# A retention layer with a gated two-layer product: queries loaded, cast and turned by pairs of chunks, their columns read as two runs

## The chip, the core and the metric

The kernel runs on one core of a Trainium2 chip. The metric is the device time of one execution in microseconds (us), lower being better; the kernel before takes 306.24 us (median of 3 runs). The core has TensorE (PE in the profile, with its weight loads as a row of their own, PEld), VectorE (DVE), ScalarE (ACT), GpSimd (POOL) and SyncE (SP), which here only issues DMAs. Each engine carries out its instructions in the order of the program and waits on semaphores for the others.

## The reference

For 8 batches, 8 heads, 576 positions and 64 dimensions per head:

```
scores = matmul(q, k^T) / sqrt(64)
ret    = scores * gamma[h] ** (i - j)   for i >= j, else 0     # gamma[h] = 1 - 2 ** (-5 - h)
x      = matmul(ret, v)                 # as [4608 positions, 512]
h      = x @ w_in                       # 512 -> 2048
out    = (h * clip(h + 3, 0, 6) / 6) @ w_out    # 2048 -> 512
```

The inputs and the output are float32; the kernel computes in float16 with float32 sums.

## The kernel before

**Work and blocks.** The 4608 positions are 9 blocks of 512. Block 0 holds the first 64 positions of all eight batches (functions with "heads" in their names); block kb >= 1 holds positions 64 to 575 of batch kb - 1, as four chunks of 128. Chunks are numbered c = 4 to 35.

**A chunk.** `load` (L167) issues three DMAs of 256 KB on SP's queue, for k, q and v, one position in a partition; four buffers of each are in rotation. `casts` (L177) makes float16 copies: ACT the keys (L185), POOL the queries and the values (L186, L187), each with the decay of its position, since gamma ** (i - j) is split into a factor for the query and one for the key. `transposes` (L190) turns keys and queries so that a head's 64 dimensions lie on the partitions. On TensorE that is eight matmuls with the identity into PSUM tiles ptk and ptq, and a copy by ACT (kT) or DVE (qT) at L198; otherwise it is one DMA transpose on SP's queue (L200). Before, queries of chunks under `PE_T` = 13 and keys of chunks under `PE_K` = 20 are turned by TensorE (L622, L636 to L638, L646).

A chunk is worked off in two steps of 64 positions. `scores` (L222) multiplies kT and qT into the PSUM tiles pa, `masked` (L241, DVE, L245) masks them, `states` (L264) multiplies keys and values into a state per step, `add` (L287) adds the states up on DVE (L290, L293) with a decay by POOL (L294), `past` (L296) copies them to float16 by ACT (L300 to L303). `cross_over` (L323) and `inner` (L327) multiply the turned queries with the past state and the masked scores with the values into the PSUM tiles po, and ACT copies po to xT (L346), which holds the block's x turned. From chunk 16 on, two chunks go together in `scores`, `states`, `cross` and `inner`.

**The two products.** `up_unit` (L446) multiplies w_in with xT in four pairs of matmuls (ph), ACT makes u (L469) and DVE g (L471). `down_plain` and, from block 2 on, `down_strassen` multiply g with w_out (pd, pm); the latter has side sums that DVE does (L486), of g and of w_out. All matmuls of the products go through `product` (L158), so they stand under L162.

**The order** of the instructions on each engine is written by hand. `go` (L649) reads plans of short codes: `c12` casts chunk 12 and fetches a later one, `t12` turns it on TensorE, `a12` are its scores, `s12` its states, `u12` adds them, `z12` copies them, `x12` are the cross products, `i12` the inner ones, `D4` four steps of the down product, `U1` an up unit, `L` and `R` up units of the left or right half of a block, `+1` a side sum. From block 2 on the tables STEADY and FIRST_STEADY say which codes follow which up unit. PSUM tiles named pp rotate through six buffers: a new one waits until the one six before it has been read.

Of the kernel before, what the change touches and what calls it, by code (L numbers as in the profile page):

```python
# [12 lines left out]
FP32 = mybir.dt.float32  # L13
FP16 = mybir.dt.float16
# [7 lines left out]
def kernel(  # L22
# [13 lines left out]
    P = 128  # L36
# [32 lines left out]
    ij = const.tile([P, NJ + 4], I32)  # L69
    fj = const.tile([P, NJ + 4], FP32)  # L70
    key, odd = fj[:, NJ + 1:NJ + 2], fj[:, NJ + 3:NJ + 4]
    arg = const.tile([P, NJ + 1, 2 * H], FP32)
    dec = const.tile([P, NJ + 1, 2 * H], FP32)
# [16 lines left out]
    def indices():  # L90
        nc.vector.memset(half, 0.5)
        nc.gpsimd.iota(ii[:, 0:NJ], pattern=[[0, NJ]], base=0, channel_multiplier=1)
        nc.gpsimd.iota(ii[:, NJ:NJ + 1], pattern=[[1, 1]], base=0, channel_multiplier=1)
        nc.gpsimd.iota(query, pattern=[[TL, 2], [1, NJ], [NJ, RP]], base=0, channel_multiplier=0,
                       allow_small_or_imprecise_dtypes=True)
        make_identity(nc, ident16)
        p_ = ii[:, NJ:NJ + 1]
        nc.vector.tensor_scalar(ij[:, 0:NJ], ii[:, 0:NJ], P - B, 1, ALU.bitwise_and, ALU.logical_shift_right)
        nc.vector.tensor_copy(ij[:, NJ:NJ + 1], p_)
        nc.vector.tensor_scalar(ij[:, NJ + 1:NJ + 2], p_, RP - 1, 2, ALU.bitwise_and, ALU.logical_shift_left)  # L100
        nc.vector.tensor_scalar(ij[:, NJ + 2:NJ + 3], p_, 5, None, ALU.logical_shift_right)
        nc.vector.tensor_scalar(ij[:, NJ + 3:NJ + 4], p_, 4, 1, ALU.logical_shift_right, ALU.bitwise_and)
        nc.vector.tensor_copy(fj, ij)
        nc.vector.tensor_tensor(fj[:, 0:NJ], fj[:, 0:NJ], query[:, 0:TL:RP], ALU.add)
        nc.vector.tensor_scalar(fj[:, NJ:NJ + 1], fj[:, NJ:NJ + 1], 1.0, -float(P // 2), ALU.mult, ALU.add)
        nc.vector.tensor_copy(by_chunk.rearrange("p (c e r) -> p c e r", c=NCB, e=2),
                              ident16.rearrange("p (r e c) -> p c e r", e=2, c=NCB))

    def distances():
        nc.vector.memset(scale, float(np.log(D ** -0.5)))  # L110
        nc.vector.tensor_tensor(key, key, fj[:, NJ + 2:NJ + 3], ALU.add)
# [12 lines left out]
    def decays():  # L124
        for h in range(H):
            lg = float(np.log(gamma[h]))
            nc.gpsimd.tensor_scalar(arg[:, :, h], fj[:, 0:NJ + 1], lg, float(np.log(D ** -0.5)),
                                    ALU.mult, ALU.add)
            nc.gpsimd.tensor_scalar(arg[:, :, H + h], fj[:, 0:NJ + 1], -lg, 0.0, ALU.mult, ALU.add)
# [13 lines left out]
    def mask_of_chunk():  # L143
        nc.gpsimd.memset(mask, 1.0)
        nc.gpsimd.affine_select(out=mask, in_=mask, compare_op=ALU.is_ge,
                                fill=0.0, base=0, pattern=[[1, P]], channel_multiplier=-1)
        nc.gpsimd.tensor_copy(mask[SUB:P, 0:SUB], mask[SUB:P, SUB:P])
# [18 lines left out]

    def load(c):  # L167
        tiles, dmas = [], []
        b, s0 = c // NCB - 1, TL + P * (c % NCB)
        for nm, src in (("k", k), ("q", q), ("v", v)):  # L170
            t = io.tile([P, H, D], FP32, tag=f"f{nm}", name=f"f{nm}{c}")
            dmas.append(nc.sync.dma_start(t, src[b, :, s0:s0 + P, :].rearrange("h s d -> s h d")))
            tiles.append(t)
        st[c] = dict(f=tiles)
        return dmas

    def casts(c):  # L177
        fk, fq, fv = st[c]["f"]
        dd = dec[:, NJ, :].unsqueeze(2).to_broadcast([P, 2 * H, D])
        k16 = work.tile([P, NP, 2, D], FP16, tag="k16", bufs=4, name=f"k16_{c}")  # L180
        q16 = work.tile([P, NP, 2, D], FP16, tag="q16", name=f"q16_{c}")
# [4 lines left out]
        nc.gpsimd.tensor_tensor(by_head(q16), in_rows(fq), in_rows(dd[:, 0:H, :]), ALU.mult)  # L186
        nc.gpsimd.tensor_tensor(v16, fv, dd[:, H:2 * H, :], ALU.mult)  # L187
        st[c].update(k16=k16, q16=q16, v16=v16)

    def transposes(c, on_pe, names="kq"):  # L190
        for nm in names:
            src = st[c][nm + "16"].rearrange("p i a d -> p (i a d)")
            dst = work.tile([P, NP, P], FP16, tag=f"{nm}T", bufs=dict(k=4, q=6)[nm], name=f"{nm}T_{c}")
            if on_pe:
                pt = psum.tile([P, NP, P], FP32, tag="pp", name=f"pt{nm}{c}")
                for i in range(NP):
                    product(pt[:, i, :], src[:, i * P:(i + 1) * P], ident16, start=True, stop=True)
                (nc.scalar.copy if nm == "k" else nc.vector.tensor_copy)(dst, pt)  # L198
            else:
                nc.sync.dma_start_transpose(dst, src)  # L200
            st[c][nm + "T"] = dst
# [9 lines left out]
    def mm(*args, **flags):  # L211
        return lambda: nc.tensor.matmul(*args, skip_group_check=True, **flags)  # L212

# [8 lines left out]
    def scores(c0):  # L222
# [6 lines left out]
        for x, c in enumerate(g):  # L229
            kT, qT = st[c]["kT"], st[c]["qT"]  # L230
# [77 lines left out]
    def cross(c0, flip):  # L308
# [5 lines left out]
        for x, c in enumerate(g):  # L314
            for i in range(NP):
                for a in range(2):
                    s, cc, b = a ^ flip, i // 2 + 2 * a, i % 2
                    todo[a].append(mm(gs[c0]["po"][s][rows(b), x, cc, :], z16s[c][rows(a), s, i, :],
                                      st[c]["qT"][rows(a), i, rows(s)],
                                      start=bool(flip) and x == 0 and i < 2, stop=False))  # L320
# [6 lines left out]
    def inner(c0):  # L327
# [16 lines left out]
        xt = xts[kb][:, :, i0 * P:i0 * P + n * P].rearrange("p n (x s q) -> p s x n q", x=n, s=2)  # L344
        for s in range(2):
            nc.scalar.copy(xt[:, s], po[s])  # L346
        for c in g:
            del st[c], z16s[c]
# [18 lines left out]
    def load_half(i, nm, e, queue, behind=None):  # L367

        if nm not in hd.setdefault(i, {}):
            if queue is nc.gpsimd:  # L370
                hd[i][nm] = heads16(i, nm)
            else:
                f = io.tile([P, H, D], FP32, tag=f"f{nm}", name=f"h{nm}{i}")
                hd[i][nm] = f.rearrange("p (e j) d -> p e j d", e=2)
# [6 lines left out]
    def heads16(i, nm):  # L381
        return work.tile([P, 2, NJ, D], FP16, tag=f"{nm}16", bufs=dict(k=4, q=3, v=NV16)[nm], name=f"h{nm}16_{i}")
# [6 lines left out]
    def turn_heads(i, nm, copy):  # L389
# [6 lines left out]
        t = work.tile([P, x, NJ, y], FP16, tag=f"{nm}T", bufs=dict(k=4, q=6)[nm], name=f"h{nm}T_{i}")  # L396
# [225 lines left out]
    PE_T, PE_K = 13, 20  # L622
# [9 lines left out]
    def cast(c):  # L632
        if c < NCH:
# [3 lines left out]
            if c >= PE_T:  # L637
                transposes(c, False, "kq" if c >= PE_K else "q")  # L638
            fetch(c + IOB + (c < PE_T - 2))

    def do(todo):
        for what, c in todo:
            if what == "+":
                side_sums(c)
            elif c < NCH:
                {"c": cast, "t": lambda c: transposes(c, True, "kq" if c < PE_T else "k"), "a": scores, "s": states, "u": add, "z": past,  # L646
# [33 lines left out]
    with tc.manual_schedule(engines={ENG.PE, ENG.DVE, ENG.Pool, ENG.Activation, ENG.SP}):  # L680
# [66 lines left out]
        for u in range(4, NFC):  # L747
# [5 lines left out]
           "x4 a5 s5 i4 u5 z5 D7 x5 D2 i5 D2 t6 L2 c7 a6 s6 u6 L3 z6 D1 t7 L3 D2 x6 a7 s7 i6 u7 z7 L3 c8 x7 D2 i7 L1 D3 "  # L753
# [70 lines left out]
```

## Time and profile before

| | |
|---|---|
| median of 3 runs | 306.24 us (305.5 to 306.63) |
| the profiled execution | 305.81 us, of which the span of the profile is 303.4 us |
| DMA queue of SP | 127552 packets, 40.65 MB |
| loads of q | 32 of 256 KB, 5.1 us each from issue to landing (median) |
| DMA transposes | 23 of queries (4.3 us to landing), 16 of keys (5.6 us) |
| DMA bytes in all | 46.95 MB, 155 GB/s over the span |

A row of a timeline gives the start, the duration of the group, the engine, the line, the operation with what it writes and reads, the number of instructions and, in brackets, how long the engine was idle before and what ended the wait. A row of the groups gives the busy time and the mean of one instruction in ns, then the idle time before. Matmuls overlap, so that eight of them in 0.26 us can start 0.09 us ahead of the next group. A row of the waits gives the sum in us, the number and the longest.

### The profile page before, as it was taken

To read this page: it belongs to the slowest core of one execution; us is meant where nothing else is said; L and a number is where in the kernel's file an instruction comes from. 1 tells how busy PE (TensorE), PEld (TensorE's weight loads), DVE (VectorE), ACT (ScalarE), POOL (GpSimd) and SP (SyncE) were. 2 spreads that over 40 slices of the span, in tenths; PEclk is the share of its full clock that TensorE was granted. 3 is DMA by queue.
4 is the path that set the end of the run, shared out by engine and by line. 5 is a ranking of instruction groups with operands and counts; after the bars stand their busy time and mean duration, and the time that the engine had idled before them with its cause. 6 is when DMAs were issued, how large, how long until landed. Compare 5 with 4: busy or idle time off the path is not lost.

```text
span 303.4 us, 12742 instructions
## 1 busy us (share of the span) xinstructions
PE 290.3 (96%) x5594; PEld 221.8 (73%) x5594; DVE 214.0 (71%) x385; ACT 196.7 (65%) x367; POOL 138.3 (46%) x176
## 2 busy tenths in 40 slices
PE   5799999999999899999999998999999999999995
PEld 2578565788655567878888776887788778787895
DVE  4729635878975668788977886779767885657554
ACT  4659965999677687675677566656755665555520
POOL 7885077607852900718633863187428203100510
PEclk9579999999999999999999999999999999999999
DMA  7999999998999999698999999999996200210113
GB/s 161 161 192 213 194 218 204 215 212 189 185 191 198 194 191 134 126 149 250 197 204 156 206 153 193 173 196 177 203 112 125 89 4 0 92 51 2 71 71 138
DMA packets 132758, 46.95 MB, mean 155 GB/s; under 512 B 121952, under 2 KB 128096, under 8 KB 132704
## 3 DMA queue, kind: packets, MB, share of 16 engines
q1 hardware_dynamic: 127552, 40.65, 75.6%
q0 software_dynamic: 4720, 5.11, 10.3%
q8 instruction: 43, 0.70, 1.1%
q10 hardware_dynamic: 432, 0.39, 0.6%
q14 instruction: 11, 0.09, 0.1%
HBM read 36.70 MB, written 9.44 MB: 152 GB/s over the span
## 4 chain that ended last, share of the span: by engine, by line
PE 87%; DVE 4%; ACT 4%; DMA 2%; issue 2%; SPq 0%; ACTq 0%; DVEq 0%
PE ph L162 38%; PE pm L162 28%; PE pd L162 9%; PE po L212 4%; PE pa L212 2%; DVE g L471 2%; DMA hq<-in_q_dram 2%; ACT u L469 1%; PE pu L212 1%; PE ptk L162 1%; PE hptq L393 1%; DVE a L245 1%; PE hpo L438 1%; ACT hqT L397 1%; ACT kT L198 1%
## 5 line engine op out<-in xcount | busy, mean ns | idle before, releaser
L162 PE MATMUL ph<-xT,win 128*64 128x512 f16 (+1 forms) x1248 | 146.7, 364 | 1.0 <-DVE z L290 0.6
L471 DVE SCALAR_TENSOR_TENSOR g<-u,ph 128x512 f16<-128x512 f32 (+1 forms) x156 | 98.3, 643 | 54.1 <-ACT u L469 53.8
L469 ACT ACTIVATE u<-ph,half 128x512 f32<-128x512 f32 (+1 forms) x156 | 100.2, 660 | 46.1 <-PE ph L162 43.4
L162 PEld LDWEIGHTS <-win 128*64 128x64 f16 x1248 | 85.4, 136 | 28.1 <-issue 2.5
L162 PEld LDWEIGHTS <-g 128*64 128x64 f16 x928 | 51.8, 110 | 14.6
L162 PEld LDWEIGHTS <-s 128*64 128x64 f16 x896 | 51.5, 110 | 8.6 <-issue 1.1
L294 POOL TENSOR_TENSOR z<-z,gpow 128x256 f32<-128x256 f32 x24 | 15.5, 646 | 76.3 <-DVE z L293 53.0
L162 PE MATMUL pm<-ws,s 128*64 128x256 f16 x672 | 46.8, 273 | 0.0
L187 POOL TENSOR_TENSOR v<-fv,dec 128x512 f16<-128x512 f32 x32 | 38.3, 1196 | 0.0
L186 POOL TENSOR_TENSOR q<-fq,dec 128x512 f16<-128x512 f32 x32 | 37.4, 1169 | 1.5 <-DMA fq<-in_q_dram 0.8
L550 POOL TENSOR_TENSOR u<-u,p 128x512 f32<-128x512 f32 x7 | 8.9, 1271 | 58.3 <-ACT u L590 52.0
L162 PE MATMUL pd<-wout,g 128*64 128x512 f16 x256 | 34.4, 382 | 0.0
L346 ACT CAST xT<-po 128x256 f16<-128x256 f32 (+1 forms) x44 | 18.6, 473 | 23.3 <-PE po L212 23.0
L162 PE MATMUL pm<-wout,g 128*64 128x256 f16 x448 | 32.0, 273 | 0.0
L245 DVE TENSOR_TENSOR a<-pa,mask 128x256 f16<-128x256 f32 (+1 forms) x44 | 21.9, 540 | 8.0 <-PE pa L212 6.6
L486 DVE TENSOR_TENSOR s<-g 128x1024 f16<-128x1024 f16 x28 | 21.5, 771 | 0.2
L185 ACT CAST k<-fk 128x512 f16<-128x512 f32 x32 | 19.9, 620 | 0.0
L300 ACT CAST z<-z 128x512 f16<-128x512 f32 x24 | 14.8, 618 | 4.7 <-DVE z L290 4.7
L162 PE MATMUL pm<-wout,s 128*64 128x256 f16 x224 | 16.7, 273 | 0.7 <-issue 0.6
L162 PE MATMUL pm<-ws,g 128*64 128x256 f16 x224 | 17.2, 274 | 0.0
L212 PE MATMUL po<-qT,z 64*64 64x64 f16 x512 | 12.4, 198 | 0.5 <-ACT z L303 0.2
L486 DVE TENSOR_TENSOR s<-g,s 128x1024 f16<-128x1024 f16 x14 | 12.7, 905 | 0.0
(109 smaller groups left out, 276.7 us busy)
## 6 DMA issues: line engine op xcount, KB each, us to landing
fk<-in_k_dram SPq DMA_DIRECT2D x32, 256.0 KB, 4.9
fq<-in_q_dram SPq DMA_DIRECT2D x32, 256.0 KB, 5.1
fv<-in_v_dram SPq DMA_DIRECT2D x32, 256.0 KB, 5.2
out_dram<-o SPq DMA_DIRECT2D x14, 512.0 KB, 4.4
wout<-in_moe_w_out_dram POOLq DMA_DIRECT2D x4, 512.0 KB, 16.9
out_dram<-o SPq DMA_DIRECT2D x7, 256.0 KB, 2.9
win<-in_moe_w_in_dram POOLq DMA_DIRECT2D x3, 512.0 KB, 10.7
hq<-in_q_dram SPq DMA_DIRECT2D x6, 128.0 KB, 5.2
```

The costliest lines, as they stand in the source:

```text
L162: nc.tensor.matmul(out[r], lhs[:, r], rhs, skip_group_check=True, **flags)
L185: nc.scalar.copy(by_head(k16), in_rows(fk))
L186: nc.gpsimd.tensor_tensor(by_head(q16), in_rows(fq), in_rows(dd[:, 0:H, :]), ALU.mult)
L187: nc.gpsimd.tensor_tensor(v16, fv, dd[:, H:2 * H, :], ALU.mult)
L212: return lambda: nc.tensor.matmul(*args, skip_group_check=True, **flags)
L245: nc.vector.tensor_tensor(a16[:, a, 0:n].rearrange("p x i q -> p (x i) q"), pa[a].rearrange("p x i q -> p (x i) q"), m, ALU.mult)
L294: nc.gpsimd.tensor_tensor(new, new, decay, ALU.mult)
L300: nc.scalar.copy(z16, zs[c])
L346: nc.scalar.copy(xt[:, s], po[s])
L469: nc.scalar.activation(uu[:, 0:n], ph[:, 0:n], ACTF.Relu, bias=half, scale=1.0 / 6.0)
L471: nc.vector.scalar_tensor_tensor(out=g[:, hf, ths, jr, :], in0=by_half(uu), scalar=1.0, in1=by_half(ph), op0=ALU.min, op1=ALU.mult)
L486: nc.vector.tensor_tensor(*pend.popleft())
```

## The change

The query load takes two chunks (c even, c + 1) in one DMA of 512 KB: partition p holds the positions 2p and 2p + 1 of the 256, so that a run in memory is 512 bytes instead of 256. POOL casts the two positions (e = 0, 1) in two instructions at the even chunk, each with its own column of decays, and then the even chunk's values; at the odd chunk it casts the values alone. The turned pair has its columns by e and then by partition, so that the 64 queries of a step are two runs of 32 columns. Scores and cross products take them in that order (`by_parity`), the mask is made for it, and ACT's copy to xT puts the positions back in their order by writing every second element.

`PE_T` becomes 14 and `PE_K` 17: TensorE turns the queries of chunks 4 to 13 (at the even chunk, both of the pair) and the keys of 4 to 16; a DMA transpose takes a pair of queries, 11 in all, and the keys of 17 to 35, 19 in all. Three places of the plan change. In the block of chunks 4 to 7, three `L` units go ahead of `z7` and one ahead of `x7`. `t13` goes ahead of `c15` and eight down steps, `t14` ahead of three up units, `t15` ahead of two up units and their down steps. Queries of block 0 share the tiles of the pairs (`half_tile`).

```diff
     def load(c):
-        tiles, dmas = [], []
+
+        dmas = []
         b, s0 = c // NCB - 1, TL + P * (c % NCB)
+        st[c] = {}
         for nm, src in (("k", k), ("q", q), ("v", v)):
-            t = io.tile([P, H, D], FP32, tag=f"f{nm}", name=f"f{nm}{c}")
-            dmas.append(nc.sync.dma_start(t, src[b, :, s0:s0 + P, :].rearrange("h s d -> s h d")))
-            tiles.append(t)
-        st[c] = dict(f=tiles)
+            if nm != "q":
+                t = io.tile([P, H, D], FP32, tag=f"f{nm}", name=f"f{nm}{c}")
+                dmas.append(nc.sync.dma_start(t, src[b, :, s0:s0 + P, :].rearrange("h s d -> s h d")))
+                st[c]["f" + nm] = t
+            elif c % 2 == 0:
+                t = io.tile([P, H, 2, D], FP32, tag="fq", bufs=2, name=f"fq{c}")
+                dmas.append(nc.sync.dma_start(t, src[b, :, s0:s0 + 2 * P, :].rearrange("h (p e) d -> p h e d", e=2)))
+                st[c]["fq"] = t
         return dmas
...
-        nc.scalar.copy(by_head(k16), in_rows(fk))
-        nc.gpsimd.tensor_tensor(by_head(q16), in_rows(fq), in_rows(dd[:, 0:H, :]), ALU.mult)
-        nc.gpsimd.tensor_tensor(v16, fv, dd[:, H:2 * H, :], ALU.mult)
+        nc.scalar.copy(by_head(k16), in_rows(st[c]["fk"]))
+        if c % 2 == 0:
+            q16 = work.tile([P, 2, NP, 2, D], FP16, tag="q16", bufs=2, name=f"q16_{c}")
+            for e in range(2):
+                nc.gpsimd.tensor_tensor(by_head(q16[:, e]), in_rows(st[c]["fq"][:, :, e, :]),
+                                        in_rows(dd[:, NJ + 1 + e, 0:H, :]), ALU.mult)
+            st[c]["q16"] = q16
+        nc.gpsimd.tensor_tensor(v16, st[c]["fv"], dd[:, NJ, H:2 * H, :], ALU.mult)
...
+            if nm == "q" and c % 2:
+                continue
+            n = dict(k=1, q=2)[nm]
...
+                for e in range(n):
+                    pt = psum.tile([P, NP, P], FP32, tag="pp", name=f"pt{nm}{c}_{e}")
+                    for i in range(NP):
+                        j = NP * e + i
+                        product(pt[:, i, :], src[:, j * P:(j + 1) * P], ident16, start=True, stop=True)
+                    (nc.scalar.copy if nm == "k" else nc.vector.tensor_copy)(dst[:, e], pt)
...
+                for x in range(2):
+                    qts[c + x] = dst[:, :, :, SUB * x:SUB * x + SUB].rearrange("p e i (s r) -> p i s e r", s=2)
...
+    by_parity = lambda t: t.rearrange("p (e r) -> p e r", e=2)
...
-                        todo[a].append(mm(pa[a][rows(s), x, i, :], kT[rows(a), i, rows(s)], qT[rows(a), i, rows(s)],
+                        todo[a].append(mm(by_parity(pa[a][rows(s), x, i, :]), kT[rows(a), i, rows(s)], qT[rows(a), i, s],
...
-        xt = xts[kb][:, :, i0 * P:i0 * P + n * P].rearrange("p n (x s q) -> p s x n q", x=n, s=2)
+        xt = xts[kb][:, :, i0 * P:i0 * P + n * P].rearrange("p n (x s r e) -> p s x n e r", x=n, s=2, e=2)
         for s in range(2):
-            nc.scalar.copy(xt[:, s], po[s])
+            nc.scalar.copy(xt[:, s], po[s].rearrange("p x n (e r) -> p x n e r", e=2))
...
-    PE_T, PE_K = 13, 20
+    PE_T, PE_K = 14, 17
...
-           "x4 a5 s5 i4 u5 z5 D7 x5 D2 i5 D2 t6 L2 c7 a6 s6 u6 L3 z6 D1 t7 L3 D2 x6 a7 s7 i6 u7 z7 L3 c8 x7 D2 i7 L1 D3 "
+           "x4 a5 s5 i4 u5 z5 D7 x5 D2 i5 D2 t6 L2 c7 a6 s6 u6 L3 z6 D1 t7 L3 D2 x6 a7 s7 i6 u7 L3 z7 c8 L1 x7 D2 i7 D3 "
...
-           "a12 s12 u12 c15 D4 z12 +1 D4 t13 x12 a13 s13 i12 u13 z13 D1",
+           "a12 s12 u12 t13 c15 D4 z12 +1 D4 x12 a13 s13 i12 u13 z13 D1",
...
-        go("U1 D3 U1 D2 U1 U1 D2 t14 x13 a14 s14 i13 u14 z14 o1 c16 U1 D2 U1 D2 U1 D2 U1 D2 +1 U1 t15 x14 a15 s15 i14 u15 z15 "
+        go("U1 D3 t14 U1 D2 U1 U1 D2 x13 a14 s14 i13 u14 z14 o1 c16 U1 D2 U1 D2 t15 U1 D2 U1 D2 +1 U1 x14 a15 s15 i14 u15 z15 "
```

More of the change, by code (lines that the diff above doesn't have):

```diff
@@ L68 @@
     ii = const.tile([P, NJ + 1], I32)
[L69 to L73, printed above, removed]
+    ij = const.tile([P, NJ + 6], I32)
+    fj = const.tile([P, NJ + 6], FP32)
+    key, odd = fj[:, NJ + 3:NJ + 4], fj[:, NJ + 5:NJ + 6]
+    arg = const.tile([P, NJ + 3, 2 * H], FP32)
+    dec = const.tile([P, NJ + 3, 2 * H], FP32)
     ident16 = const.tile([P, P], FP16)
@@ L110, in distances @@
         nc.vector.memset(scale, float(np.log(D ** -0.5)))
-        nc.vector.tensor_tensor(key, key, fj[:, NJ + 2:NJ + 3], ALU.add)
+        nc.vector.tensor_tensor(key, key, fj[:, NJ + 4:NJ + 5], ALU.add)
         nc.vector.scalar_tensor_tensor(out=key, in0=odd, scalar=float(TL), in1=key, op0=ALU.mult, op1=ALU.add)
@@ L190, in transposes @@
+        nc.gpsimd.tensor_tensor(v16, st[c]["fv"], dd[:, NJ, H:2 * H, :], ALU.mult)
+        st[c].update(k16=k16, v16=v16)
     def transposes(c, on_pe, names="kq"):
         for nm in names:
-            src = st[c][nm + "16"].rearrange("p i a d -> p (i a d)")
-            dst = work.tile([P, NP, P], FP16, tag=f"{nm}T", bufs=dict(k=4, q=6)[nm], name=f"{nm}T_{c}")
-            if on_pe:
[L195 to L198, printed above, removed]
-            else:
-                nc.sync.dma_start_transpose(dst, src)
@@ L206 @@
+            if nm == "k":
+                st[c]["kT"] = dst[:, 0]
+            else:
+                for x in range(2):
+                    qts[c + x] = dst[:, :, :, SUB * x:SUB * x + SUB].rearrange("p e i (s r) -> p i s e r", s=2)
+    qts = {}
     PAIRS = 16
@@ L229, in scores @@
         for x, c in enumerate(g):
-            kT, qT = st[c]["kT"], st[c]["qT"]
+            kT, qT = st[c]["kT"], qts[c]
             for i in range(NP):
@@ L372, in load_half @@
             else:
-                f = io.tile([P, H, D], FP32, tag=f"f{nm}", name=f"h{nm}{i}")
-                hd[i][nm] = f.rearrange("p (e j) d -> p e j d", e=2)
+                f = half_tile(io, "fq", i, FP32, "hq", bufs=2) if nm == "q" else io.tile(
+                    [P, H * D], FP32, tag=f"f{nm}", name=f"h{nm}{i}")
+                hd[i][nm] = f.rearrange("p (e j d) -> p e j d", e=2, j=NJ)
         d = queue.dma_start(hd[i][nm][:, e].rearrange("p j d -> p (j d)"),
@@ L395, in turn_heads @@
         x, y = (NCB, 2 * RP) if nm == "k" else (2 * NCB, RP)
-        t = work.tile([P, x, NJ, y], FP16, tag=f"{nm}T", bufs=dict(k=4, q=6)[nm], name=f"h{nm}T_{i}")
+        t = half_tile(work, "qT", i, FP16, "hqT", bufs=3) if nm == "q" else work.tile(
+            [P, H * D], FP16, tag="kT", bufs=4, name=f"hkT{i}")
+        t = t.rearrange("p (x j y) -> p x j y", x=x, j=NJ)
         copy(t, pt.rearrange("p j (x y) -> p x j y", y=y))
@@ L645, in do @@
             elif c < NCH:
-                {"c": cast, "t": lambda c: transposes(c, True, "kq" if c < PE_T else "k"), "a": scores, "s": states, "u": add, "z": past,
+                {"c": cast, "t": lambda c: transposes(c, True, "kq" if c < PE_T else "k" if c < PE_K else ""), "a": scores, "s": states, "u": add, "z": past,
                  "x": cross_over, "i": inner, "k": keys_heads, "h": head_states, "o": lambda _: store(*kept.popleft())}[what](c)
```

50 lines of the change are left out of this document (31 added, 19 removed).

## The prediction, made before the changed kernel had run

> **What bounds the kernel now.** I read the page first, then the table by stretches, then who waited for whom, then the timelines of TensorE (PE), VectorE (DVE) and ScalarE (ACT) around each wait. The first two lines are the page's busy times and its chain, then come two stretches (length, then busy time of PE, weight loads, DVE, ACT and POOL, granted clock, DMA share, GB/s), and three waits.
>
> ```profile
> PE 290.3 (96%) x5594; PEld 221.8 (73%) x5594; DVE 214.0 (71%) x385; ACT 196.7 (65%) x367; POOL 138.3 (46%) x176
> ...
> PE 87%; DVE 4%; ACT 4%; DMA 2%; issue 2%; SPq 0%; ACTq 0%; DVEq 0%
> ```
> ```profile
> 60.00:70.00 10.00, 9.30 (x221) 7.88 (x225) 7.92 (x21) 9.65 (x25) 2.51 (x4) 1.00 0.98 209
> ```
> ```profile
> 90.00:115.00 25.00, 23.66 (x380) 15.05 (x378) 15.69 (x27) 18.64 (x36) 9.90 (x11) 1.00 1.28 194
> ```
> ```profile
> POOL q L186 <- DMA fq<-in_q_dram: 0.8, 2, 0.6
> ...
> DVE hq L386 <- DMA hq<-in_q_dram: 2.6, 1, 2.6
> ```
> ```profile
> PE pa L212 <- ACT kT L198: 1.8, 3, 0.8
> ```
>
> PE is 96% busy and carries 87% of the chain: the kernel is bound by the number of PE instructions, and what else there is to win is PE's idle time. From 60 to 70 us ACT is busy for 9.65 of 10 and sets the pace. From 90 to 115 us PE idles 25.00 - 23.66 = 1.34 us, at full clock, and nearly all of it is one kind: scores that wait for ACT to copy a turned key (three waits, 1.8 us, two of them in this stretch). The DMA share of 1.28 looks alarming, yet GpSimd (POOL) waited for queries only 0.8 us in all. So fewer or longer query loads win nothing by themselves: I cost the new loads at nothing, hidden by loads that land ahead of their casts.
>
> **Term 1: the three waits for turned keys.** The change issues the turns of keys 13, 14 and 15 some units earlier. The rows are the cross products (po) and the scores (pa) behind them: first a pair without a wait, then the three with one.
>
> ```profile
> 76.06 0.26 PE L212 MATMUL po<-qT,z 64*64 64x64 f16 x8
> 76.15 0.30 PE L212 MATMUL pa<-qT,kT 64*64 64x64 f16 x16
> ...
> 87.09 0.26 PE L212 MATMUL po<-qT,z 64*64 64x64 f16 x8
> 87.83 0.32 PE L212 MATMUL pa<-qT,kT 64*64 64x64 f16 x16 [0.49 <-ACT kT L198]
> ...
> 93.93 0.26 PE L212 MATMUL po<-qT,z 64*64 64x64 f16 x8
> 94.68 0.32 PE L212 MATMUL pa<-qT,kT 64*64 64x64 f16 x16 [0.49 <-ACT kT L198]
> ...
> 101.67 0.26 PE L212 MATMUL po<-qT,z 64*64 64x64 f16 x8
> 102.78 0.32 PE L212 MATMUL pa<-qT,kT 64*64 64x64 f16 x16 [0.85 <-ACT kT L198]
> ```
>
> Without a wait the scores follow after 0.09 us. They follow after 0.74, 0.75 and 1.11 us at chunks 13, 14 and 15, so 0.65, 0.66 and 1.02 us are to be had. At chunk 13 something else is late next: the cross products there need the state that DVE adds, and DVE now casts two turned query tiles before that instead of one.
>
> ```profile
> 80.80 2.60 DVE L486 TENSOR_TENSOR ws<-wout,ws 128x1024 f16<-128x1024 f16 x2
> 83.45 0.69 DVE L198 CAST qT<-ptq 128x512 f16<-128x512 f32 x1
> 84.06 0.79 DVE L486 TENSOR_TENSOR ws<-wout 128x1024 f16<-128x1024 f16 x1
> ...
> 86.16 0.41 DVE L290 TENSOR_TENSOR z<-pa,zh 128x256 f32<-128x256 f32 x1
> ```
> ```profile
> 86.61 0.41 ACT L303 CAST z<-z 128x256 f16<-128x256 f32 x1 [0.26 <-DVE z L290]
> ```
>
> DVE runs without a gap here: the cast of 83.45 makes room at 84.06, so a second one costs 0.61. The add of 86.16 becomes 86.77, ACT's copy ends at 87.02 + 0.61 = 87.63, and the cross products of 87.09 start at about 87.70; the scores then at 87.79 against 87.83. Behind this new wait on PE stand the scores, states and inner products of chunks 12 and 13. So chunk 13 yields 0.04, and **term 1 is -(0.04 + 0.66 + 1.02) = -1.72**.
>
> **Term 2: turns that leave PE.** The keys of chunks 17, 18 and 19 go to the DMA; chunk 13's query comes onto PE, but under the wait just named, so it costs nothing there (0.22 if that wait were gone).
>
> ```profile
> 42.97 0.40 PE L162 MATMUL ptk<-ident,k 128*64 128x128 f16 x8
> 43.19 0.40 PE L162 MATMUL ptq<-ident,q 128*64 128x128 f16 x8
> ...
> 44.60 0.32 PE L212 MATMUL pa<-qT,kT 64*64 64x64 f16 x16
> ...
> 47.75 0.26 PE L212 MATMUL po<-qT,z 64*64 64x64 f16 x8 [0.20 <-ACT z L303]
> ```
>
> One turn of eight matmuls takes 43.19 - 42.97 = 0.22, and in the later stretch PE has no slack that would swallow it: **term 2 is -3 x 0.22 = -0.66**.
>
> **Term 3: two queries turned at once in front of the scores.** At chunk 4 PE turns key, query and now a second query, and DVE casts both before the scores may start.
>
> ```profile
> 43.62 0.69 DVE L198 CAST qT<-ptq 128x512 f16<-128x512 f32 x1 [1.13 <-PE ptq L162]
> ...
> 52.29 0.69 DVE L198 CAST qT<-ptq 128x512 f16<-128x512 f32 x1 [2.34 <-PE ptq L162]
> ```
> ```profile
> 53.05 0.32 PE L212 MATMUL pa<-qT,kT 64*64 64x64 f16 x16
> ...
> 55.30 0.41 PE L162 MATMUL ptq<-ident,q 128*64 128x128 f16 x8
> 55.66 1.53 PE L162 MATMUL ph<-xT,win 128*64 128x256 f16 x24
> ...
> 58.20 1.53 PE L162 MATMUL ph<-xT,win 128*64 128x256 f16 x24
> 59.91 0.26 PE L212 MATMUL po<-qT,z 64*64 64x64 f16 x8 [0.18 <-ACT z L300]
> ...
> 67.57 1.99 PE L162 MATMUL ph<-xT,win 128*64 128x256 f16 x32 [0.58 <-DVE z L290]
> ```
>
> Chunk 4: casts at 43.62 and 44.23, the second ends at 44.92, the scores go at 44.97 instead of 44.60: +0.37. That chunk 5's turn is shorter by 0.22 doesn't pay it back, since the cross products of 47.75 wait for a state that hangs on these scores. Chunk 6: casts at 52.29 and 52.90, the second ends at 53.59, scores at 53.64 instead of 53.05: +0.59; chunk 7's missing query returns 0.22, and the turn of 55.30 that lasts 0.36 instead of 0.22 (a PSUM tile not yet free) 0.14 more: +0.23. From chunk 8 on, three up units or an add stand between, and I count nothing.
>
> **Term 4: an order changed around chunk 7.** ACT copies the state after three activations instead of before them.
>
> ```profile
> 59.24 0.62 ACT L300 CAST z<-z 128x512 f16<-128x512 f32 x1 [0.27 <-DVE z L290]
> 59.76 1.20 ACT L469 ACTIVATE u<-ph,half 128x256 f32<-128x256 f32 x3
> ```
>
> The third activation needs the matmuls that end at 58.20 + 1.53 = 59.73; with its 0.40 (a third of 1.20) the copy starts at about 60.15, ends at 60.77, and the cross products of 59.91 go at about 60.80: +0.89. One up unit (1.53 / 3 less overlap, about 0.44) now stands ahead of them, net +0.45. Later chunk 9's query no longer takes a PSUM tile, so the wait of 0.58 at 67.57 should go: -0.57. **Terms 3 and 4: 0.37 + 0.23 + 0.45 - 0.57 = +0.48.**
>
> **Costed at nothing.** Three more tiny DVE instructions at the start hide under the 2.6 us wait for the first query; the wider decays and the mask lie in POOL's idle time. POOL casts both chunks of a pair at the even chunk, then its values: two casts in a row, the same number in all.
>
> ```profile
> L186 POOL TENSOR_TENSOR q<-fq,dec 128x512 f16<-128x512 f32 x32 | 37.4, 1169 | 1.5 <-DMA fq<-in_q_dram 0.8 <-PE po L212 0.7
> ```
> ```profile
> 83.91 2.92 SPq L200 DMA_TRANSPOSE qT<-q  x1
> ```
> ```profile
> qT<-q SPq DMA_TRANSPOSE x23, 4.3
> ```
>
> The values and the state decay queued behind come 1.2 us later at even chunks and earlier at odd ones; POOL is 46% busy. On SP's queue a transpose now waits for both casts, with the next loads behind it. Chunk 14's issue at 83.91 took 2.92; doubled 5.8, and 4.3 to land behind it at worst: 94.0, just where the scores at 94.68 - 0.7 want it. I take no wait there.
>
> Two costs are not in the trace: TensorE streams a query as two runs of 32 columns, and ACT writes xT at every second element.
>
> ```profile
> L406 PE MATMUL hpk<-hk,by_chunk 128*32 128x128 f16 x64 | 1.6, 222 | 0.0
> ...
> L162 PE MATMUL ptq<-ident,q 128*64 128x128 f16 x72 | 3.6, 219 | 0.0
> ...
> L346 ACT CAST xT<-po 128x256 f16<-128x256 f32 x24 | 7.8, 376 | 6.6 <-PE po L212 6.3
> ```
>
> Line 406 streams two runs of 64 and takes 222 ns, one run of 128 takes 219: 0 to 3 ns for each of 1024 matmuls, 0 to 3.1 us; I take 0, the end that line 406 is nearest to. The xT copy: 0, or twice its 376 ns; that would be on the path only where ACT is full, six copies about the stretch from 60 to 70 us, 0 to 2.3 us; I take 0. Neither can gain, as the elements are the same.
>
> **Sum**: -1.72 - 0.66 + 0.48 = -1.90. The profiled execution took 305.81 and would take 303.9; the median of the runs, 306.24, lies 0.43 higher: **304.3 us**.
>
> **The rivals.**
> (a) The waits are only passed on: ACT is full from 60 to 70 us, and freed PE time after 94 us meets the next copy of theirs. Then terms 1 and 3 cancel and term 2 or less is left: 305.6 to 306.5. For it speaks chunk 13, where it happens; against it the gaps of ACT and DVE after 90 us (DVE 15.69 of 25).
> (b) Slower: the two runs of columns cost TensorE. From 2 ns for each of 1024 matmuls the gain is gone, from 3.4 ns it is slower by over 0.5%. If each run counted as a matmul of its own, at 0.09 / 8 = 11 ns, it would be +11.5: 315.8. Against it speaks line 406.
> [...]
> (c) Chunk 14's queries land late in the crowded queue: the 0.66 of chunk 14 is lost and up to a us more: 304.3 + 0.66 to 304.3 + 1.66, about 305 to 306.
> (d) More: chunk 13 gives its 0.65 after all (303.7), and with 16 loads less a quarter of the chain's issue gaps goes too (2% of 303.4 is 6.1): 302.2 to 303.7.
>
> **How the numbers follow.** Forecast 0.51, (a) 0.24, (b) 0.13, (c) 0.05, (d) 0.07. 0.5% of 306.24, about what a measurement of this kernel tells from no change, is 1.5 us: faster means below 304.7, slower above 307.8. The forecast's own range is 303.3 to 305.2, so 0.44 of its 0.51 is faster, with (d) 0.51; same 0.07 + 0.24 + 0.05 = 0.36; slower 0.13. The range from 302.0 to 306.6 leaves out (b).
>
> **What would show it.** No row of scores with a wait for a turned key after 85 us; the cross products near 87 us with a wait for ACT's state copy; 24 matmuls fewer that turn keys (ptk) and 8 more that turn queries (ptq); about 0.4 us of new idle time near 45 and 54 us and 0.9 near 60, none near 67.6; pa and po no longer than before, and the copy of line 346 still at 376. Wrong: scores of chunks 14 to 17 that wait for a DMA, longer pa or po, or activations queued behind each other after 100 us.

## The result and the profile after

| | median, us | lowest to highest | runs | ratio to before, 95% interval |
|---|---|---|---|---|
| before | 306.33 | 305.50 to 306.63 | 4 | |
| changed | 302.54 | 302.52 to 303.87 | 4 | 0.9891 [0.9859, 0.9924] |
| changed, measured again beside its parts | 302.93 | 302.51 to 304.21 | 6 | 0.9907 [0.9876, 0.9938] (before there: 305.60, 25 runs) |

The change makes the kernel about 1% faster, 2.7 to 3.8 us, where 1.9 were forecast. A profiled execution of 302.57 us with a span of 300.6 is read here; before it was 305.81 with 303.4. Ratios leave disturbed runs out and are not formed from the two medians, so they can differ from the medians' ratio.

The page of the changed kernel, busy times and chain of waits:

```profile
PE 289.0 (96%) x5578; PEld 222.2 (74%) x5578; DVE 213.7 (71%) x389; ACT 197.9 (66%) x364; POOL 135.4 (45%) x176
...
PE 78%; DMA 10%; ACT 3%; DVE 2%; POOL 2%; issue 2%; SPq 1%; ACTq 0%
```

TensorE (PE) still is the bound, with 16 products fewer. Its waits in the changed kernel, by who ended them (sum in us, times, longest), and its two stretches (length, then busy time of PE, weight loads, DVE, ACT and POOL, clock, DMA share, GB/s):

```profile
PE pd L168 <- ACT o L556: 1.3, 2, 0.7
...
PE po L246 <- ACT z L336: 0.6, 1, 0.6
PE ph L168 <- ACT xT L382: 0.6, 1, 0.6
...
PE pa L246 <- DVE qT L226: 0.3, 1, 0.3
```
```profile
60.00:70.00 10.00, 9.10 (x213) 7.59 (x208) 7.57 (x19) 9.38 (x23) 1.00 (x3) 1.00 0.94 212
90.00:115.00 25.00, 24.86 (x389) 17.16 (x385) 16.98 (x30) 19.34 (x38) 10.04 (x11) 1.00 0.76 147
```

The wait of scores (pa) for a turned key is gone, and from 90 to 115 us PE idles 0.14 us in place of 1.34. New or longer are waits for ScalarE (ACT): for its copy of a finished output (o), of a state (z) and of xT. Around chunk 7, and at the scores of chunks 13 to 15:

```profile
57.93 0.33 PE L168 MATMUL ph<-xT,win 128*64 128x256 f16 x2
58.87 1.86 PE L168 MATMUL ph<-xT,win 128*64 128x256 f16 x30 [0.60 <-ACT xT L382]
61.36 0.25 PE L246 MATMUL po<-qT,z 64*64 64x64 f16 x8 [0.63 <-ACT z L336]
...
68.52 1.55 PE L168 MATMUL ph<-xT,win 128*64 128x256 f16 x24 [0.26 <-DVE z L326]
...
87.97 0.84 PE L168 MATMUL pd<-wout,g 128*64 128x512 f16 x6 [0.60 <-ACT o L556]
88.73 0.26 PE L246 MATMUL po<-qT,z 64*64 64x64 f16 x8
88.82 0.30 PE L246 MATMUL pa<-qT,kT 64*64 64x64 f16 x16
...
94.92 0.26 PE L246 MATMUL po<-qT,z 64*64 64x64 f16 x8
95.01 0.30 PE L246 MATMUL pa<-qT,kT 64*64 64x64 f16 x16
...
102.03 0.26 PE L246 MATMUL po<-qT,z 64*64 64x64 f16 x8
102.11 0.30 PE L246 MATMUL pa<-qT,kT 64*64 64x64 f16 x16
```

All three scores follow their cross products (po) after 0.09 us now. The operations themselves (mean ns is the last number ahead of the second bar):

```profile
L382 ACT CAST xT<-po 128x512 f16<-128x512 f32 x20 | 13.4, 741 | 16.4 <-PE po L246 16.4
...
L246 PE MATMUL po<-qT,z 64*64 64x64 f16 x512 | 12.5, 198 | 1.1 <-ACT z L336 0.6 <-ACT z L339 0.4
...
L382 ACT CAST xT<-po 128x256 f16<-128x256 f32 x24 | 9.2, 454 | 5.6 <-PE po L246 5.6
...
L246 PE MATMUL pa<-qT,kT 64*64 64x64 f16 x512 | 8.5, 195 | 0.5 <-DVE qT L226 0.3 <-DVE g L512 0.2
```

Products with two runs of columns last what they did (195 and 198 ns; 196 and 198 before). The copies of xT do not: 454 ns where it was 376, and 741 where it was 588.

**Where the time went.** To find the place of a difference I cut each trace at a score product of certain chunks (the first one of a chunk, but the ninth one of chunk 9 and of the pairs from 16 on; the same one in all kernels), so that the same work is compared whatever came earlier. Chunk 4 is counted from the start of the span; times in us, one profile each, up to the last score product's pair (34); behind it all kernels take 56.17 or 56.18 to PE's last product.

| kernel | to 4 | 4 to 9 | 9 to 13 | 13 to 16 | 16 to 20 | 20 to 34 |
|---|---|---|---|---|---|---|
| before | 44.60 | 25.41 | 17.83 | 28.93 | 22.51 | 104.59 |
| changed | 44.06 | 26.63 | 18.12 | 27.59 | 21.68 | 102.86 |
| difference | -0.54 | +1.22 | +0.29 | -1.34 | -0.83 | -1.73 |
| changed again | 45.48 | 26.62 | 18.12 | 27.61 | 22.63 | 102.18 |
| pairs alone | 45.05 | 26.70 | 17.99 | 28.93 | 22.47 | 103.69 |
| pairs and early turns | 45.90 | 26.63 | 18.13 | 28.06 | 22.55 | 103.16 |
| early turns alone | 45.42 | 25.42 | 17.96 | 27.92 | 22.88 | 103.22 |
| turns alone | 44.58 | 25.42 | 17.96 | 28.12 | 21.70 | 105.88 |
| turns alone, again | 43.93 | 25.40 | 19.89 | 27.45 | 21.89 | 105.44 |
| changed, xT contiguous | 46.01 | 26.44 | 18.12 | 27.76 | 22.61 | 101.57 |
| changed, old order at 7 | 45.77 | 26.70 | 18.12 | 27.74 | 22.60 | 101.58 |
| changed, halves | 44.38 | 25.81 | 18.12 | 27.47 | 22.58 | 102.54 |
| halves, xT contiguous | 44.87 | 25.73 | 18.12 | 27.68 | 21.97 | 102.98 |
| halves, old order at 7 | 45.19 | 25.63 | 18.12 | 27.66 | 21.67 | 102.30 |
| changed, later stream | 44.96 | 26.84 | 18.13 | 27.68 | 21.77 | 104.04 |

From chunk 4 to 16 kernels with the same program there agree within some hundredths to some tenths, so single profiles can be used there (the 19.89 holds a wait for a DMA, read below). Behind chunk 16 they don't: the two profiles of the changed kernel differ by 0.95 from 16 to 20. The start is another matter: kernels whose start is the same program reach chunk 4 anywhere between 44.06 and 46.01 us, so the 0.54 that the changed kernel seems to win there is chance. What is left is a loss of 1.51 up to chunk 13 and a win of 3.90 behind it, 1.73 of which lie where nothing was forecast. The second profile shows 2.41 there, but nothing of the 0.83.

### The profile page after: what moved, and what is told of

Read it like the earlier page. It is cut to its first block, busy times and chain, and to the rows that moved or that the text cites. A ratio compares the mean times of both kernels' runs of the same rounds, so it can differ in the third digit from the quotient of the medians.

```text
span 300.6 us, 12679 instructions
## 1 busy us (share of the span) xinstructions
PE 289.0 (96%) x5578; PEld 222.2 (74%) x5578; DVE 213.7 (71%) x389; ACT 197.9 (66%) x364; POOL 135.4 (45%) x176
## 4 chain that ended last, share of the span: by engine, by line
PE 78%; DMA 10%; ACT 3%; DVE 2%; POOL 2%; issue 2%; SPq 1%; ACTq 0%
PE ph L168 35%; PE pm L168 29%; PE pd L168 6%; DMA wout<-in_moe_w_out_dram 6%; PE po L246 4%; DMA hk<-in_k_dram 3%; PE pa L246 2%; DMA fk<-in_k_dram 2%; POOL win L658 1%; PE pu L246 1%; DVE g L512 1%; ACT u L510 1%; PE ptk L168 1%; POOL hv L412 1%; ACT k L203 1%
## 5 line engine op out<-in xcount | busy, mean ns | idle before, releaser
L168 PE MATMUL ph<-xT,win 128*64 128x512 f16 (+1 forms) x1248 | 145.1, 364 | 1.5 <-ACT xT L382 0.6
L168 PEld LDWEIGHTS <-s 128*64 128x64 f16 x896 | 50.3, 110 | 8.1 <-issue 0.2
L168 PE MATMUL pm<-ws,s 128*64 128x256 f16 x672 | 45.5, 273 | 0.0
L382 ACT CAST xT<-po 128x256 f16<-128x256 f32 (+1 forms) x44 | 22.5, 584 | 22.0 <-PE po L246 22.0
L210 POOL TENSOR_TENSOR v<-fv,dec 128x512 f16<-128x512 f32 x32 | 35.1, 1101 | 1.3 <-DMA fv<-in_v_dram 1.3
L527 DVE TENSOR_TENSOR s<-g 128x1024 f16<-128x1024 f16 x28 | 20.0, 716 | 0.2
L246 PEld LDWEIGHTS <-z 64*64 64x64 f16 x512 | 8.0, 106 | 7.7 <-ACT z L336 1.8
```

Source lines behind the costliest of these rows:

```text
L168: nc.tensor.matmul(out[r], lhs[:, r], rhs, skip_group_check=True, **flags)
L210: nc.gpsimd.tensor_tensor(v16, st[c]["fv"], dd[:, NJ, H:2 * H, :], ALU.mult)
L382: nc.scalar.copy(xt[:, s], po[s].rearrange("p x n (e r) -> p x n e r", e=2))
L527: nc.vector.tensor_tensor(*pend.popleft())
```

## The experiments

**Which part carries the gain.** The changed kernel with the old orders and with keys 17 to 19 on TensorE:

```diff
-    PE_T, PE_K = 14, 17
+    PE_T, PE_K = 14, 20
-  "... i6 u7 L3 z7 c8 L1 x7 D2 i7 D3 "   "... u12 t13 c15 D4 z12 +1 D4 x12 ..."   (and t14, t15)
+  "... i6 u7 z7 L3 c8 x7 D2 i7 L1 D3 "   "... u12 c15 D4 z12 +1 D4 t13 x12 ..."
```

> Pairs of queries alone: loaded, cast, turned and read in pairs as in the change, but the plan of the kernel before (turns of keys 13 to 15 and the state copy of chunk 7 where they were) and PE_K = 20. Theory S (the gain is the earlier key turns and the three key turns less on TensorE; the pairs themselves cost a little): 306.8 to 308.0, 0.5 to 1.7 above the kernel before, with the three waits for turned keys back (1.8 us). Theory D (the longer query loads, half the packets, bring most of it: an earlier start and fewer gaps late in the run): 303.5 to 305.

Measured: 306.63 (12 runs) beside 306.43, ratio 1.0007 [0.9976, 1.0038]. Queries by two bring nothing. That rules out D; by S it would have been 0.5 to 1.7 us above the kernel before, and it is 0.2. The kernel before, with the turns of 13 to 15 early and keys 17 to 19 turned by DMA:

```diff
-    PE_T, PE_K = 13, 20
+    PE_T, PE_K = 13, 17
-  "... c15 D4 z12 +1 D4 t13 x12 ..."   "U1 D3 U1 D2 U1 U1 D2 t14 x13 ..."   "... D2 +1 U1 t15 x14 ..."
+  "... t13 c15 D4 z12 +1 D4 x12 ..."   "U1 D3 t14 U1 D2 U1 U1 D2 x13 ..."   "... t15 U1 D2 U1 D2 +1 U1 x14 ..."
```

> The kernel before with only the earlier turns of keys 13, 14 and 15 and PE_K = 17; queries stay single, one DMA each. S: 306.3 - 0.65 - 0.66 - 1.02 - 0.66 = 303.3, since chunk 13's second query cast on VectorE isn't there. D: not below 304.8, and the start of the run and its second half as in the kernel before.

Measured: 305.14 (12 runs), 0.9970 [0.9936, 1.0004]. Less than S expected. The same without the DMA turns (only the three orders changed):

> The kernel before with only the earlier turns of keys 13, 14 and 15; PE_K stays 20. S: 306.3 - 2.33 = 304.0, 0.7 above the run with PE_K = 17. D: 305 to 306.

Measured: 306.19 (12 runs), 0.9960 [0.9918, 1.0002]; by the medians, 306.19 and 306.43, it is only 0.1%. So the parts brought 0 and at most 0.4%, with 1 inside every interval, and the whole 1.1%: either the whole was lucky, or it is more than its parts. The whole and the turns alone were run again, unaltered:

> The changed kernel a second time, unaltered, beside its parts on one chip. Theory A, the parts add up: queries by two bring nothing (306.6 against 306.4 before) and the keys' turns alone 1.0 us, so the whole stands at 305.0 to 305.5 and the 302.5 of its first four runs were a lucky draw. Theory I, the whole is more than its parts: the turns moved to the queues need the room that the halved query loads make there, so 302.5 to 303.5. The first score product, at 44.06 us in the first profile of this kernel, comes anywhere between 44 and 46 us, since the same start gave 45.05 with the pairs alone and 46.01 with contiguous writes.

> The kernel before with the keys' turns of 13 to 15 early and keys 17 to 19 turned by DMA, queries as before; the same as in the run of the turns alone. Both theories: 305.0 to 305.5 again. They differ in the profile: by I, TensorE waits once or more for a load or a DMA turn (1.6 us for turned queries of the pair 24 in its first profile); by A, that wait was one bad draw and is not seen again.

Measured: the whole 0.9907 [0.9876, 0.9938], so A fell; the turns alone 304.25 (12 runs), 0.9932 [0.9906, 0.9959]. By their medians the two runs of the turns alone agree (0.9958 and 0.9956 of the kernel before); both gain less than the whole, though the interval of the second overlaps that of the whole. The traces of the turns alone (first the first one, then the second) show a cause, at the scores of chunks 22 and 23 (the expectation calls it the pair 24); the 16 products of chunk 22 have gone, those of chunk 23 wait for its turned queries:

```profile
155.57 0.32 PE L212 MATMUL pa<-qT,kT 64*64 64x64 f16 x16 [1.60 <-DMA qT<-q]
```
```profile
156.44 0.32 PE L212 MATMUL pa<-qT,kT 64*64 64x64 f16 x16 [1.77 <-DMA qT<-q]
```

PE comes earlier, and the queue with 23 turns of queries and 19 of keys is not ready. The second one also waited 1.77 us at chunk 13, its first queries turned by DMA (its profiled execution took 305.81, more than its median of 304.25, so such waits need not be as long in all). In none of the eight profiles with queries by two and keys from 17 on turned by DMA is there such a wait: there one transpose turns two chunks, and the odd one's queries come with the even one's. So queries by two bring nothing by themselves, but with more turns on the queue they keep it ahead; whether by their loads or by their fewer transposes was not separated. That these waits are the whole of the difference between 0.9932 or 0.9970 and 0.9907 was not tried.

**What the three key turns are worth.** The changed kernel with only this put back:

```diff
-    PE_T, PE_K = 14, 17
+    PE_T, PE_K = 14, 20
```

> The changed kernel with keys 17 to 19 back on TensorE: queries by two, the new order, the early turns of 13 to 15, without the three turns by DMA. By A the difference to the whole is what three key turns cost TensorE, 0.66 us by the forecast, so 305.7 to 306.2. By I it lies 0.5 to 1.5 above the whole, 303.5 to 304.5, because the room on the queues is there and only the three turns come back.

Measured: 305.93 (12 runs), 1.0003 [0.9974, 1.0031], against 0.9907 for the whole. So taking three key turns from TensorE is worth 1.0%, 3 us, over four times the 0.66 of the forecast, and more than A (0.66) or I (0.5 to 1.5) gave it. The traces show the 0.66 in part: from 16 to 18 keys 18 and 19 leave 11.03 - 10.61 = 0.42; key 17's turn lies from chunk 15 to 16, where a wait for DVE differs as well. Behind chunk 20, where none of these turns stands, the changed kernel takes 0.30 and 0.98 us less in its two profiles; the rest is not located. From chunk 18 on PE's idle times are of a kind for which the profile names no releaser, or (at 173.70) an activation. In brackets the idle time; the kernel before, then pairs and early turns:

```profile
173.70 1.08 PE L162 MATMUL ph<-xT,win 128*64 128x512 f16 x8 [0.32 <-ACT u L469]
...
186.00 0.19 PE L212 MATMUL po<-a,v 64*64 64x64 f16 x1 [0.82 <-issue]
...
219.31 0.95 PE L162 MATMUL pm<-wout,s 128*64 128x256 f16 x14 [0.57 <-issue]
```
```profile
131.22 0.22 PE L246 MATMUL po<-a,v 64*64 64x64 f16 x3 [0.25 <-issue]
...
175.31 0.63 PE L168 MATMUL pm<-wout,g 128*64 128x256 f16 x8 [0.66 <-issue]
```

Counted in PE's own order, such gaps stood in all kernels ahead of product 2397, 2653, 2909, 3292, 3548, 4186 or 4442 (one more or less), whatever the product was; once also ahead of 862. These numbers lie 128 or a multiple of it apart, but for one or two. Each product has a weight load (5578 of each on the page of the changed kernel), so that is every 256 instructions, and the page of the changed kernel has a queue that loads 43 pieces of 0.70 MB / 43 = 16 KB:

```profile
q8 instruction: 43, 0.70, 1.0%
```

The times of the pieces in the traces say more. One piece comes in for about each 128 products (43 for the 5578 of the changed kernel). All 29 gaps of this kind of 0.15 us or more, behind 44 us in the 14 profiles, end 1.3 to 1.8 us after the end of the last piece that came in: in the changed kernel 228.34 behind 226.88, in the kernel before 173.70 behind 172.34 (so this one is of the same kind, though an activation is named) and 186.00 behind 184.65. I read this as PE waiting for its next instructions; no row of the profile names that. Of the 29, 23 stand where the 128 products before took only 1.8 to 3.8 us, the other six where they took 4.0 to 5.4; where they took longer, no gap follows. So it may matter which work stands between two such numbers, and a shift of the stream changes that. The changed kernel with 24 small products (12 calls of two each) ahead of all that counts:

```diff
+        for _ in range(small):
+            product(idle[:, 0, 0:16], ident16, ident16[:, 0:16], start=True, stop=True)
...
-        idle_products(3)
+        idle_products(3, 6)
-        idle_products(1)
+        idle_products(1, 6)
```

> The changed kernel with 12 more idle products of 16 columns, 24 products and 24 weight loads, at two places of the first 9 us where TensorE waits for heads; its instruction stream is then as long as that of the kernel with queries by two and early turns, and all that follows stands 24 products further back in it. What is to be told apart: why the three key turns are worth 3.0 us (302.9 against 305.9) and not 0.66. Theory B: TensorE's gaps without a releaser lie at fixed numbers of its stream (product 3292 and 3548 in the four kernels that turn keys 17 to 19 on TensorE, 0.3 to 1.3 us in sum 0.5 to 1.5; none above 0.24 there in nine profiles without them), so what counts is which work stands at these numbers; then the gaps at 3292 and 3548 come back and the stretches from chunk 24 to 26 to 28 take 15.0 to 15.5 and 14.7 to 15.9 us in place of 14.63 and 14.38, and the time is 303.6 to 304.6. Theory N: the gaps hang on the turns themselves or the queues' traffic; then the two stretches stay at 14.6 and 14.4 and the time at 302.5 to 303.4.

Measured: 306.39 (12 runs) beside 306.75, 0.9994 [0.9967, 1.0020]. **All of the gain is gone.** (The changed kernel itself was not run beside it, and only this one shift was tried.) The stretches from chunk 24 to 26 and to 28 took 15.41 and 14.71 us (14.63 and 14.38 in the changed kernel; 15.49 and 14.72 with pairs and early turns, whose stream is as long). The small products themselves (in the groups of 18 and 14), and the gaps:

```profile
4.83 1.77 PE L168 MATMUL idle<-ident 128*64 128x512 f16 x18
...
7.68 0.60 PE L168 MATMUL idle<-ident 128*64 128x512 f16 x14
...
141.28 0.23 PE L246 MATMUL po<-a,v 64*64 64x64 f16 x5 [0.63 <-issue]
...
174.01 0.63 PE L168 MATMUL pm<-wout,g 128*64 128x256 f16 x8 [0.56 <-issue]
```

In the changed kernel the same two groups, without the small products, take 1.49 and 0.43, so the 24 cost at most 0.28 + 0.17 = 0.45 us, and chunk 4 is reached at 44.96, within the others' range. The gap at product 3292 came back (0.56); at 3548 a product starts 0.31 us behind the one before it, where the same work of the changed kernel has 0.01. New is one of 0.20 at product 862, in the stretch from chunk 4 to 7. The gaps stayed at their numbers while the work moved by 24: theory B holds by place, and N is out. By size B is too small: it gave 303.6 to 304.6, and the gaps of 0.15 us or more behind chunk 4 sum to 1.39 us here against 0.54 and 0.93 in the two profiles of the changed kernel, 0.5 to 0.9 of the 2.7 us that were lost. In single profiles the stretch from 20 to 34 shows 104.04 against 101.57 to 102.98 in the seven other profiles with queries by two and these turns on the queue, 1.1 to 2.5 of the 2.7 us (0.87% of 306), in part without a gap that the profile shows; the rest is not located.

**Where the loss around chunk 7 comes from.** Contiguous writes of xT, with ACT reading PSUM at every 32nd element instead:

```diff
-  xt = ....rearrange("p n (x s r e) -> p s x n e r", x=n, s=2, e=2)
-  nc.scalar.copy(xt[:, s], po[s].rearrange("p x n (e r) -> p x n e r", e=2))
+  xt = ....rearrange("p n (x s r e) -> p s x n r e", x=n, s=2, e=2)
+  nc.scalar.copy(xt[:, s], po[s].rearrange("p x n (e r) -> p x n r e", e=2))
```

> The changed kernel, but ScalarE's copy to xT goes through its elements in the order of the output: it writes xT without gaps and reads PSUM at every 32nd element, where the changed kernel reads without gaps and writes every second element. If the writes at every second element are what made the copy 454 and 741 ns (376 and 588 before), it is back at 376 to 390 and 588 to 600 here and the wait for the xT copy near 58.9 us goes: 0.5 to 1.5 faster than the changed kernel, 301.0 to 302.0. If the copy is slow whichever side has the gaps: 302.5.

Measured: 304.11 (9 runs), 0.9929 [0.9896, 0.9961]: no better than the whole, and the wait for xT stays (0.50 us at 60.71). The copies are what they were before, so it was the spaced writes that cost them their 78 and 153 ns:

```profile
L382 ACT CAST xT<-po 128x512 f16<-128x512 f32 x20 | 10.7, 589 | 16.0 <-PE po L246 16.0
...
L382 ACT CAST xT<-po 128x256 f16<-128x256 f32 x24 | 7.8, 378 | 5.6 <-PE po L246 5.6
```

But the stretch from chunk 7 to chunk 9 only went from 13.49 to 13.30 (12.37 before). The order was tried next:

```diff
-  "... i6 u7 L3 z7 c8 L1 x7 D2 i7 D3 "
+  "... i6 u7 z7 L3 c8 x7 D2 i7 L1 D3 "
```

> The changed kernel with the old order around chunk 7 (the past of chunk 7 ahead of the piece of the down product, not behind it). If the new order is what cost 1.7 us around chunk 7 in the changed kernel, this is 0.8 to 1.5 below the whole of the same call; if the queries by two cost it (the pairs alone, in the old order, took 9.07 us from the scores of chunk 6 to those of chunk 8, and the whole 9.01), it is within 0.4 of the whole.

Measured: 304.23 (8 runs), 0.9939 [0.9907, 0.9971], 1.3 us above the whole by the medians, with intervals that overlap; 13.56 us from chunk 7 to 9. Not the order. Left is the wait for xT at 58.87. In the program it stands at the third matmul of a unit of the left half: the first quarter of xT's depth is read at once, the second waits for the copy of chunk 6, which writes the other half of the positions. The kernel before has no wait at this product. With the block laid out in two halves, that copy lies outside what the left half reads, whatever its pattern:

```diff
+    halves = lambda t: t.rearrange("p n b -> p (n b)").rearrange("p (h n c) -> p h n c", h=2, c=HB)
...
+        i1 = i0 % 2 if kb == 1 else i0
+        xin = halves(xts[kb])[:, i0 // 2] if kb == 1 else xts[kb]
-        xt = xts[kb][:, :, i0 * P:i0 * P + n * P].rearrange(...)
+        xt = xin[:, :, i1 * P:i1 * P + n * P].rearrange(...)
...
-            product(ph[:, 0:n], w[...], xts[kb][:, dmc, cols], ...
+            product(ph[:, 0:n].rearrange("p (a t) -> p a t", t=HB), w[...],
+                    halves(xts[kb])[:, ths, dmc] if kb == 1 else ...
```

> The changed kernel with the block of chunks 4 to 7 laid out in two halves of 256 positions in xT, so that the copies of chunk 6 write a stretch that the up products of the left half don't read. Theory F: the changed kernel's 0.60 us wait for a copy of xT at the third left unit behind chunk 6 is for positions that its product doesn't read (the copy's five-dimensional pattern is taken for the whole stretch from its first to its last element); then that wait goes, the wait of 0.63 for the past of chunk 7 shrinks with it, and the scores of chunk 7 to those of chunk 9 take 12.3 to 12.9 us in place of 13.48, whatever the random gaps later do; the time is 0.6 to 1.2 below the whole, near 302.0 where the whole gave 302.9. Theory W: the wait is for the copy's own length (454 in place of 376 ns); then the stretch stays at 13.3 to 13.5 and the time at that of the whole.

> The halves and the contiguous writes of xT together (copies of 376 and 588 ns again). By F the stretch from chunk 7 to chunk 9 is that of the halves alone or up to 0.2 shorter (the contiguous writes alone took 0.18 from it), and the time within 0.4 of the halves alone; by W it is 0.2 below the whole, from the shorter copies alone.

> The halves with the old order around chunk 7. By F the old order then costs what the forecast gave it: no wait of 0.63 behind the left units, but 0.58 again behind the turns of chunk 9 or half of it, so the stretch is within 0.3 of that of the halves alone. By W it stays at 13.5.

Measured, beside 305.71 (23 runs): halves 303.26 (12 runs), 0.9931 [0.9898, 0.9964]; with contiguous writes 302.96 (12 runs), 0.9915 [0.9888, 0.9941]; with the old order 302.37 (6 runs), 0.9898 [0.9856, 0.9941]. From chunk 7 to 9: 12.67, 12.59 and 12.49 us. Around chunk 7 with the halves, then with the halves and the old order:

```profile
58.25 1.97 PE L168 MATMUL ph<-xT,win 128*64 128x256 f16 x32
60.85 0.25 PE L246 MATMUL po<-qT,z 64*64 64x64 f16 x8 [0.64 <-ACT z L336]
```
```profile
59.05 1.53 PE L168 MATMUL ph<-xT,win 128*64 128x256 f16 x24
60.90 0.26 PE L246 MATMUL po<-qT,z 64*64 64x64 f16 x8 [0.32 <-ACT z L336]
```

The wait for xT is gone and theory F holds by place: the wait was for positions that the product does not read. The wait for the state of chunk 7 did not shrink in the new order (0.64) as F expected, but is half as long in the old one. The times of the halves are not below the whole's by more than the intervals; the version with the old order, with the shortest span of the profiled executions (300.2 us), is the best here by its median, and equal to the changed kernel within error.

## Why the prediction was right, and where it was not

The direction was right and the time lay in the range of 302.0 to 306.6, below the 303.3 to 305.2 of the forecast itself. The sum was not right: the mechanism of terms 1 and 2 was, term 3 came out smaller, term 4 with the other sign, and what made up for it was a gain that the sum did not have. That the time is as near as it is was luck.

- **Term 1 (-1.72): -1.34 from chunk 13 to 16, nothing ahead of it.** Chunk 14 gave 6.85 - 6.19 = 0.66, chunk 15 8.09 - 7.11 = 0.98, as forecast. Chunk 13 gave nothing (3.33 us from chunk 12 to 13, 3.20 before), but not for the reason named: with early turns alone, where VectorE (DVE) casts one query tile and not two, it gave nothing either (17.96 against 17.83 from chunk 9 to 13). The wait for ACT's state copy near 87 us that was forecast is not there. What is late next is ACT's copy of an output, behind which the down product stands for 0.60 us:

```profile
87.95 0.84 PE L162 MATMUL pd<-wout,g 128*64 128x512 f16 x6 [0.60 <-ACT o L515]
88.72 0.26 PE L212 MATMUL po<-qT,z 64*64 64x64 f16 x8
```

  And from chunk 15 to 16 0.32 us came back, although key 17's turn of 0.22 left: rival (a) in small. In nine of the eleven other profiles with early turns PE waits 0.15 to 0.54 us there for DVE's g.
- **Term 2 (-0.66): right in what it counted**, 0.42 for keys 18 and 19 where they stood. Chunk 13's query, put at nothing under a wait that did not come, costs its 0.22 (from chunk 11 to 12 5.54 us in place of 5.32). The term missed that 24 products less also move all later work in PE's stream.
- **Term 3 (+0.37 + 0.23): measured +0.10** from chunk 4 to 7 (0.59 - 0.49); chunk 7's missing query returned more than 0.22. Chunk 4's own delay cannot be told apart from a start that varies by 2 us.
- **Term 4 (0.45 - 0.57 = -0.12): measured +1.12** from chunk 7 to 9. This is the step that failed. The wait of 0.58 that should go kept 0.26 (at 68.52, for the same add). The order itself is worth little either way (13.56 and 13.49, or 12.49 and 12.67 with the halves). What was left out is that the new write pattern of xT makes a product wait for positions that it does not read: 0.8 us with the new order, 1.07 with the old.
- **Costed at nothing.** Two runs of columns: right (195 and 198 ns, 196 and 198 before), rival (b) is void. Chunk 14's queries: right, no wait for a DMA in PE's rows, rival (c) is void too. The copy of xT: wrong in length (454, not 376), nearly right on the path as far as its length goes (0.19 and 0.08 us in the two pairs of runs). The 0 that the sum takes for it was my estimate, which no run shows: in the runs the copy took 78 ns longer for 256 elements and 153 ns longer for 512, and with contiguous writes it took 378 and 589 ns. The loads: right for the pairs alone (1.0007); but with the turns moved to the queue the waits of 1.6 to 1.8 us that PE has with single queries are absent.
- **Rival (d) had the size** (302.2 to 303.7) but not the cause: chunk 13 gave nothing, and the issue gaps did not go because there are 16 loads less, since the pairs alone kept them (1.62 us in sum) and the time (1.0007). They shrank from 1.71 us before to 0.54 and 0.93, and with the stream of the changed kernel shifted they are 1.39 again: for these gaps it is the place of the work that counts.

What stays open: why such a gap comes in one execution and not in the next (product 2397 had 0.69 us in one profile of the changed kernel and none in the other), and where the larger part of the 3 us lies that the three turns are worth and that the shift takes back.

## What to carry to other kernels

Before crediting a gain of 1% to what an edit does, shift the instruction stream by as many instructions where the engine idles and see whether the gain stays; here it did not (0.9994 of the kernel before, against 0.9907). Cut the traces at the same piece of work to see which stretch changed, since stretches without a wait of that kind repeat to hundredths (18.12 or 18.13 us from chunk 9 to 13 in nine profiles here) where whole executions differ by one per cent (304.01 to 307.91 us in 25 of the kernel before). And where a write gets a finer pattern, look in the trace for new waits of readers of other parts of the same tile (0.60 us for xT here, gone with the halves), and lay the parts out one behind the other.

## What the hardware showed beyond that

- ACT's copy to xT that writes 16-bit elements at every second place took 454 ns for 256 elements and 741 for 512 in the changed kernel, where the contiguous one before took 376 and 588; reading PSUM at every 32nd element instead, it took 378 and 589.
- TensorE's idle times without a releaser stood at the same numbers of its instruction stream in these 14 profiles, but for one or two 256 instructions or a multiple apart, 0.2 to 1.3 us each, and ended 1.3 to 1.8 us after a piece of 16 KB had come in on the instruction queue.
- Executions of one kernel spread more than its profile tells: 32 of the kernel before, beside the first experiments, lay between 303.52 and 309.33 us, a spread of three times the forecast's gain.
